# Moving a load ring's slots by 32 bytes in SBUF: from 992 to 0 past a multiple of 1 KB

## The chip, the cores and the metric

One core of a Trainium2 chip. The metric is the device time of one execution, in microseconds; a time quoted is the median of several executions. Most executions of one kernel lie within 0.3% of each other. A page of the profile covers about 2 us less than the device time (191.7 for 193.6).

## The reference, cut to what matters

One decode step of a mixed block: attention of 8 sequences over the last 1024 cached keys and values of 8 heads (16 query heads of 256), an MLP, and a gate that mixes both. What matters here is bytes: keys and values are 67 MB, all data 77.7 MB, and each byte is used once.

```python
W = min(4096, max(256, Sk // 4))                       # 1024
k = jnp.repeat(k_cache[:, :, Sk - W:, :], rep, axis=1)
v = jnp.repeat(v_cache[:, :, Sk - W:, :], rep, axis=1)
p = _softmax(jnp.einsum("bhqd,bhkd->bhqk", q, k) * (Dh ** -0.5), axis=-1)
o = jnp.einsum("bhqk,bhkd->bhqd", p, v)
# ... projection by wo, layernorm + MLP by w1 and w2, g * a + (1 - g) * b
```

## The kernel before

Everything large comes in through a ring of nine slots of 16 KB in each of the 128 partitions. One queue issues the loads in a fixed order, as slots come free: keys of unit 0, wq, w1, w2, then keys and values by turns (2 MB each: 128 rows of 16 KB, one per partition), wo last. Small things go to a pool `consts` that is laid out ahead of the ring in each partition.

```python
    SLOT = 8192            # bf16 elements: 16 KB
    RING = 9
    consts = ctx.enter_context(tc.tile_pool(name="consts", bufs=1))
    ring = ctx.enter_context(tc.tile_pool(name="ring", bufs=RING))
    ktpool = ctx.enter_context(tc.tile_pool(name="ktpool", bufs=3))
    # ... (cut)
    def pump():
        while len(slots) < min(len(plan), consumed[0] + RING):
            t = ring.tile([P, SLOT], BF16, tag="slot", name="slot")
            plan[len(slots)](t)
            slots.append(t)

    def done(n=1):
        consumed[0] += n
        pump()

    def kv_loader(src, u, parts):
        # ... (cut)
        def load(t):
            n = NCK * Dh // parts
            for i in range(parts):
                nc.sync.dma_start(
                    t[:, i * n : (i + 1) * n], v[:, :, i * n : (i + 1) * n]
                )
        return load
    # ... (cut)
    x_sb = consts.tile([NB, D], BF16)
    pump()
    nc.scalar.dma_start(x_sb[:], xf)
    gw_b = consts.tile([NB, D], BF16)
    # ... some forty more small tiles of consts (cut)
```

In the built program all of `consts` lies below the ring, and the slots begin at 44000, 60384, ... 175072 in each partition: 992 past a multiple of 1024, or 224 past a multiple of 256.

## Time and profile before

| | before |
|---|---|
| time, median of 3 | 193.72 us |
| span of the profile | 191.7 us |
| DMA engines busy, 46 to 164 us | 1.00 to 1.01 |
| stream, 46 to 164 us | 426 to 427 GB/s |
| last load lands | 187.1 us |
| VectorE busy, TensorE busy | 67%, 69% |

The views are shown and read in the prediction below. Beside them I use the records of single DMA packets in the trace: one per row moved, with its size, start and duration. Two durations must be kept apart: the recorded one (614 ns for most 16 KB rows), and the spacing of rows on one engine, a few ns less because records overlap.

### The profile page before, as it was taken

To read this page: it belongs to the slowest core of one execution; us is meant where nothing else is said; L and a number is where in the kernel's file an instruction comes from. 1 tells how busy PE (TensorE), PEld (TensorE's weight loads), DVE (VectorE), ACT (ScalarE), POOL (GpSimd) and SP (SyncE) were. 2 spreads that over 40 slices of the span, in tenths; PEclk is the share of its full clock that TensorE was granted. 3 is DMA by queue.
4 is the path that set the end of the run, shared out by engine and by line. 5 is a ranking of instruction groups with operands and counts; after the bars stand their busy time and mean duration, and the time that the engine had idled before them with its cause. 6 is when DMAs were issued, how large, how long until landed. Compare 5 with 4: busy or idle time off the path is not lost.

```text
span 191.7 us, 2514 instructions
## 1 busy us (share of the span) xinstructions
PE 132.8 (69%) x1017; PEld 69.4 (36%) x1026; DVE 128.6 (67%) x189; ACT 45.1 (24%) x93; POOL 5.0 (3%) x7
## 2 busy tenths in 40 slices
PE   0046899894877578865657589958684989386671
PEld 0031783441434243423232254414331534154260
DVE  7867265995949494949494949494959585876201
ACT  2031220214040404140404003403140044045101
POOL 8100000000000000000000000000000000000000
PEclk9999999999699965999999658979998599999555
DMA  5999999999999999999999999999999999999970
GB/s 196 416 412 439 423 419 432 420 420 438 431 420 434 417 427 434 420 427 431 420 434 429 417 431 427 427 427 420 431 427 420 434 427 424 431 426 415 406 307 3
DMA packets 6702, 77.85 MB, mean 406 GB/s; under 512 B 913, under 2 KB 1186, under 8 KB 1954
## 3 DMA queue, kind: packets, MB, share of 16 engines
q1 hardware_dynamic: 6496, 77.67, 96.1%
q8 instruction: 8, 0.13, 0.3%
q10 hardware_dynamic: 194, 0.02, 0.1%
q14 instruction: 4, 0.03, 0.0%
HBM read 77.68 MB, written 0.01 MB: 405 GB/s over the span
## 4 chain that ended last, share of the span: by engine, by line
DMA 96%; SPq 1%; issue 0%; PE 0%; ACT 0%; DVEq 0%; DVE 0%; ACTq 0%
DMA slot<-in_A_k_cache_dram 77%; DMA slot<-in_A_wo_dram 12%; DMA slot<-in_A_wq_dram 7%; SPq L118 1%; SPq L134 0%; PE A_ps L684 0%; ACT res L707 0%; DVEq L735 0%; DVE res L705 0%; ACTq L707 0%
## 5 line engine op out<-in xcount | busy, mean ns | idle before, releaser
L364 DVE STREAM_TRANSPOSE kt<-slot 128x2048 int32<-128x2048 int32 x32 | 73.7, 2305 | 34.6 <-DMA slot<-in_A_k_cache_dram 34.6
L436 PE MATMUL S<-kt,qw 128*128 128x512 bf16 x256 | 70.6, 422 | 30.5 <-DVE kt L364 26.9
L436 PEld LDWEIGHTS <-qw 128*128 128x128 bf16 x256 | 26.6, 104 | 68.0 <-issue 47.9
L541 ACT ACTIVATE oT<-fin,gg_s 128x16 bf16<-128x16 f32 x16 | 5.3, 329 | 76.8 <-PE fin L538 76.8
L465 ACT ACTIVATE E<-S,nmx 128x1024 bf16<-128x1024 f32 x16 | 22.3, 1392 | 2.8 <-DVE nmx L462 2.8
L508 PE MATMUL PO<-slot,ET 128*16 128x512 bf16 x256 | 20.0, 441 | 1.1 <-DMA slot<-in_A_v_cache_dram 1.1
L448 DVE TENSOR_REDUCE mx<-S 128x1 f32<-128x1024 f32 x16 | 19.0, 1184 | 0.0
L517 ACT ACTIVATE first<-PO,own 128x256 f32<-128x256 f32 x16 | 7.6, 474 | 30.2 <-PE PO L508 30.2
L478 DVE STREAM_TRANSPOSE ET<-E 128x512 int32<-128x512 int32 x16 | 11.2, 697 | 2.2 <-ACT E L465 2.2
L456 PE MATMUL mz<-m,same 128*128 128x4 f32 x32 | 6.6, 278 | 5.5 <-ACT oT L541 5.4
L430 PE MATMUL S<-place,foreign 128*128 128x512 bf16 x23 | 9.0, 390 | 0.1
L489 PEld LDWEIGHTS den<-rowsum,rowden 128*128 128x128 f32 x32 | 7.0, 223 | 3.7 <-issue 1.4
L456 PEld LDWEIGHTS mz<-m,same 128*128 128x128 f32 x32 | 5.4, 211 | 7.4 <-ACT oT L541 6.6
L508 PEld LDWEIGHTS <-ET 128*16 128x16 bf16 x256 | 5.5, 94 | 6.4 <-issue 3.3
L430 PEld LDWEIGHTS <-foreign 128*128 128x128 bf16 x32 | 3.2, 100 | 9.4 <-issue 7.6
L489 PE MATMUL den<-rowsum,rowden 128*128 128x1 f32 x32 | 5.0, 226 | 0.4 <-ACT E L465 0.4
L421 DVE CAST qw<-qp 32x512 bf16<-32x512 f32 x4 | 2.7, 687 | 3.4 <-ACT qw L419 3.4
L500 ACT ACTIVATE rsel<-sel,rb 128x8 f32<-128x8 f32 x16 | 4.7, 291 | 1.0 <-DVE rb L499 1.0
L378 PE MATMUL Sq<-slot,xT 128*8 128x512 bf16 x32 | 3.9, 616 | 1.2 <-DMA slot<-in_A_wq_dram 1.2
L684 PE MATMUL A_ps<-slot,oP 128*8 128x112 bf16 x128 | 3.8, 290 | 1.3 <-DMA slot<-in_A_wo_dram 1.3
L462 DVE TENSOR_REDUCE nmx<-mz 128x1 f32<-128x4 f32 x16 | 2.3, 143 | 3.1 <-PE mz L456 3.1
L294 POOL MEMSET qw<- 128x5120 bf16 x1 | 4.4, 4367 | 0.0
(142 smaller groups left out, 90.4 us busy)
## 6 DMA issues: line engine op xcount, KB each, us to landing
slot<-in_A_v_cache_dram SPq DMA_DIRECT2D x16, 2048.0 KB, 37.2
slot<-in_A_k_cache_dram SPq DMA_DIRECT2D x15, 2048.0 KB, 39.1
slot<-in_A_wo_dram SPq DMA_DIRECT2D x3, 896.0 KB, 32.4
slot<-in_A_k_cache_dram SPq DMA_DIRECT2D x2, 1024.0 KB, 7.3
slot<-in_A_wq_dram SPq DMA_DIRECT2D x1, 2048.0 KB, 11.5
slot<-in_B_w_dram SPq DMA_DIRECT2D x1, 1568.0 KB
slot<-in_B_w_dram SPq DMA_DIRECT2D x1, 1344.0 KB
slot<-in_A_wq_dram SPq DMA_DIRECT2D x1, 1024.0 KB, 13.4
```

The lines of the kernel that those rows point to most:

```text
L364: nc.vector.transpose(kt[:].rearrange("p c k x r -> p (c k x r)").bitcast(WORD), kn[:, hf * CH * Dh : (hf + 1) * CH * Dh].bitcast(WORD),)
L430: nc.tensor.matmul(S[u][:, cols], lhsT=foreign[:], rhs=place[:], start=True, stop=False)
L436: nc.tensor.matmul(S[u][:, cols], lhsT=qw[:, j, u, m * RQ : m * RQ + P], rhs=kt[:, :, k, :, par], start=False, stop=(k == NK - 1 and par = ...
L448: nc.vector.reduce_max(mx[:], S[u][:], axis=AXIS.X)
L456: nc.tensor.matmul(mz[:], lhsT=same[:], rhs=m4[:], start=True, stop=True)
L465: nc.scalar.activation(E[:].rearrange("p c x i -> p c i x"), S.pop(u)[:].rearrange("p (c i x) -> p c i x", i=PAIR, x=BLK), ACT.Exp, bias=n ...
L478: nc.vector.transpose(ET[:].rearrange("p c r i -> p (c r i)").bitcast(WORD), E[:].rearrange("p c x i -> p (c x i)").bitcast(WORD),)
L489: nc.tensor.matmul(den[u][:], lhsT=rowden[:], rhs=rowsum[:], start=True, stop=True)
L500: nc.scalar.activation(rsel[u][:], sel2[:], ACT.Copy, scale=rb[:])
L508: nc.tensor.matmul(PO[32 * t : 32 * t + PAIR * RQ], lhsT=ET[:, c, 0:RQ, :], rhs=vn[:, PAIR * c * Dh : PAIR * (c + 1) * Dh], start=(c < QUA ...
L517: nc.scalar.activation(first[:], PO[:, 0, :], ACT.Copy, scale=own[:, 0:1])
L541: nc.scalar.activation(oT[:, half * RQ : (half + 1) * RQ, :, b].rearrange("p h j -> p j h"), sm[:], ACT.Copy, scale=gg_s[:, 1 + b : 2 + b],)
```

## The change

The intent is that rows written by the loads begin at an even address. A tile of 32 B that nobody uses is put first in `consts`, so the ring begins at 44032 = 43 x 1024. A side effect: every other tile in `consts` and behind the ring moves by 32 B too.

```diff
+    consts.tile([P, 16], BF16, name="pad")
     x_sb = consts.tile([NB, D], BF16)
     pump()
```

## The prediction

> **What bounds the kernel now.** I read four views in this order: the strip of 40 slices, the chain of work that ended last, the waits, and the same figures by stage. The strip first, because it tells at a glance whether one resource is full throughout.
>
> ```profile
> PE   0046899894877578865657589958684989386671
> DVE  7867265995949494949494949494959585876201
> DMA  5999999999999999999999999999999999999970
> GB/s 196 416 412 439 423 419 432 420 420 438 431 420 434 417 427 434 420 427 431 420 434 429 417 431 427 427 427 420 431 427 420 434 427 424 431 426 415 406 307 3
> DMA packets 6702, 77.85 MB, mean 406 GB/s; under 512 B 913, under 2 KB 1186, under 8 KB 1954
> ```
>
> The reader is to see that the row of the 16 DMA engines is at 9 tenths from the second slice to the thirty-eighth, and that no compute engine is. From the chain of waits:
>
> ```profile
> ## 4 chain that ended last, share of the span: by engine, by line
> DMA 96%; SPq 1%; issue 0%; PE 0%; ACT 0%; DVEq 0%; DVE 0%; ACTq 0%
> DMA slot<-in_A_k_cache_dram 77%; DMA slot<-in_A_wo_dram 12%; DMA slot<-in_A_wq_dram 7%; SPq L118 1%; SPq L134 0%; PE A_ps L684 0%; ACT res L707 0%; DVEq L735 0%; DVE res L705 0%; ACTq L707 0%
> ```
>
> 96% of the span is loads into the ring that follow one another. The last load lands at 187.13 us in the same chain told in order of time; only 4.6 us (191.7 less 187.1) of last matmuls, copies and the output's store come after it. The waits say who is kept waiting, and the stages how full the stream is (the columns after the busy times are the granted TensorE clock, the DMA engines' busy share and GB/s):
>
> ```profile
> DVE kt L364 <- DMA slot<-in_A_k_cache_dram: 34.6, 14, 2.8
> ...
> PE S L436 <- DVE kt L364: 26.9, 12, 3.1
> ```
>
> ```profile
> 46.00:85.00 39.00, 29.12 (x167) 14.04 (x168) 28.04 (x32) 9.31 (x20) 0.00 (x0) 0.87 1.00 426
> 85.00:125.00 40.00, 28.37 (x166) 13.86 (x168) 28.28 (x33) 9.31 (x20) 0.00 (x0) 0.87 1.00 426
> 125.00:164.00 39.00, 29.11 (x166) 14.04 (x168) 27.81 (x33) 9.29 (x20) 0.00 (x0) 0.87 1.01 427
> ```
>
> VectorE's transposes of the keys wait for keys, TensorE's scores wait for the transposes, and from 46 to 164 us the stream runs at 426 to 427 GB/s with the engines busy all the time. So the time is what the 16 DMA engines take per byte, and a change matters only if it changes that.
>
> **What the Trainium skill says.** "DMA: Bandwidth & Descriptors", section "Where 436 GB/s comes from", puts the ceiling at 16 ports x 32 B x 850 MHz = 435.2 GB/s. The trace's 426 to 427 is 98% of it: about 2% is lost and nothing more can be won. The same page, section "How a descriptor splits into AXI transactions", says that a descriptor goes out in transactions of 256 B, each of which must start at a multiple of 256 B; one that starts 224 B past such a multiple first costs a full transaction of which 32 B are used, and a shorter leftover at the end. "SBUF — State Buffer", section "Operand start alignment", says that its rule on starts is about what is legal and that its runs timed nothing. The same page, section "SBUF: two separate sides", says that DMA and engine ports do not contend; nothing in this trace speaks against it, as the stages above show one rate while the engines' load varies.
>
> **The change, part by part.** It declares a tile of 16 bf16 (32 B in each partition) that no instruction reads or writes. The instruction order of the built program is the same on TensorE but for numbers in names, and no instruction, wait or DMA is added: the counts of the groups will be the same. What moves is addresses. In the built programs the nine slots begin at 44000 + 16384 i in each partition before, and at 44032 + 16384 i after; 44000 is 42 x 1024 + 992, or 224 B past a multiple of 256; 44032 is 43 x 1024. All 275 other listed tiles' addresses, uses of the slots included, rise by 32 B too. The sources in HBM stay where they were.
>
> First the most that it can bring if the skill's account of split transactions holds for the write side as it stands. A row of 16384 B is 512 beats of 32 B. Started 224 B past a multiple of 256 it would be 8 (the first transaction) + 63 x 8 + 7 = 519 beats. A beat at 850 MHz is 1.18 ns, so 7 beats are 8.2 ns per row. The trace's packet records on the load queue have 4096 rows of 16384 B, 384 of 8192, 384 of 7168, and 128 each of 12544, 10752, 4096, 3584, 2688, 1792 and 896 B, 5760 in all and 360 for each of 16 engines: 360 x 8.2 ns = 2.96 us. It would all lie on the path that sets the end, as 96% of that path is loads. 193.72 - 2.96 = 190.8 us, 1.5% less. That is an upper estimate, by that page.
>
> Then whether the records look as if those 7 beats were paid. The usual time of one packet in the trace is 614 ns for 16384 B, 309 for 8192, 159 for 4096, 74 for 1792 and 41 for 896. Without any loss they would be 602.4, 301.2, 150.6, 65.9 and 32.9 (bytes / 27.2 per ns): 7.8 to 8.4 ns more in the last four, which looks just like 7 beats. But a packet's record overlaps the next: two successive starts on one engine lie some 3 to 4 ns closer than the recorded time (613 ns recorded, 609 between starts; 74 recorded, 70 between starts). So the cost of a short packet is nearer 4 ns than 8, less than 7 beats of 1.18. And the trace holds a comparison of its own: the eight rows of gate_w, 896 B each, land at 17408 = 17 x 1024, a whole multiple of 1 KB, and each took 41 ns; the last pieces of wo, also 896 B, begin 96 B past a multiple of 256 (and their source 128 B past one), and 120 of 128 took 41 ns as well. An aligned start has saved nothing there. I take from this that writes into SBUF pay for the bytes, and a small fixed cost, wherever they start. The weakness of this comparison is that gate_w is read from one row over and over, and that 896 B say little about rows of 16 KB.
>
> What the 16 KB rows have beyond twice a row of 8 KB is left: 614 - 602.4 = 11.7 against 7.8 ns, 3.9 ns more. If the crossed boundaries cause that part alone, it is 256 rows per engine x 3.9 ns = 1.0 us. In about a quarter of these packets 621 ns are seen instead, some two of the eight that an engine moves for one load; that goes with the jump in partition and source after four rows, and a shift of all starts by 32 B leaves the jump in place.
>
> The sum, by my main reading: 0 us from the stream, 0 from instructions, so 193.7 us. Weighed with the other cases below it comes to 193.5.
>
> **Rivals.** (1) Split transactions are paid on the write side: 190.8 us as worked out. For it: 426 x 519 / 512 = 432, close under the ceiling, so the lost 2% would be mostly explained. Against it: the 896 B rows, and the 1792 B rows whose spacing of 70 ns is 60 beats where 63 would be due. (2) Only long rows pay, 1.0 us: 192.7. For it is only that the 16 KB rows are worse than twice 8 KB; against it, that the source's jumps explain such things as well. (3) The moved engine operands get slower or faster. Every one was at a multiple of 32 B before and is at one after, so I expect 2305 ns for the keys' transposes again; and if they were 5% slower (32 x 0.115 = 3.7 us of VectorE), VectorE waits 34.6 us for keys and has that room: 193.7. (4) A worse pattern, with more writes of one moment in the same part of the memory, now that rows begin evenly: slots are 16384 B apart before as after, and the rows of all partitions start at one offset in both, so the pattern only moves; it would cost, and nothing in the profile asks for it.
>
> **Range and chances.** No change seen, 193.5 to 193.9: some 72%. Rival 2 or a part of it, 192.2 to 193.4: 14%. Rival 1, 190.5 to 191.5: 9%. The rest is slower by a little or something unknown. Eight times in ten that gives 191.4 to 194.0. Faster by over 2% means under 189.85, so 3.87 us from the stream of about 185 us; at 426.5 GB/s that needs 426.5 x 185 / 181.1 = 435.6, above the ceiling: 2%. Slower by over 2% needs a loss for which I see no source: 1%. Within 2%: 97%.
>
> **What would show each step right or wrong.** Right: 426 to 427 GB/s again from 46 to 164 us, 614 ns for most 16 KB packets, 309 for 8 KB ones, the chain still 96% loads with the last landing near 187.1 us, keys' transposes at 2305 ns. The gate_w rows, which lose their even start (17440 after the change), stay at 41 ns. Rival 1 would show 605 to 606 ns for 16 KB and a stream near 432 GB/s, rival 2 some 610 ns and 429. A time under 190 us would mean that the ceiling is not what holds the stream; one above 195 that placement in SBUF costs writes or reads in a way that I don't see.

## The result, and the profile after

| | before | after |
|---|---|---|
| time, median (range) | 193.69 us (193.35 to 193.83), 4 runs | 191.52 us (191.41 to 191.56), 4 runs |
| after / before | | 0.989 (95%: 0.987 to 0.991) |
| once more, on another occasion | 193.41 us, 9 runs | 191.68 us, 5 runs; 0.991 (0.990 to 0.993) |

A ratio here is the mean time of one kernel's fast runs over that of the other's fast runs of the same rounds, so it isn't quite the ratio of the medians. The gain is about 1%, some 1.7 to 2.2 us: inside the 2% band, and clear of noise.

The profile after, in the same views. The strip:

```profile
DMA  5999999999999999999999999999999999999980
GB/s 195 417 432 426 428 439 427 432 425 425 442 425 435 425 425 439 425 439 429 425 432 427 439 429 422 439 425 435 429 425 439 429 429 429 429 434 421 415 338 4
```

The chain of waits:

```profile
## 4 chain that ended last, share of the span: by engine, by line
DMA 81%; PE 9%; DVE 6%; SPq 1%; ACT 1%; issue 1%; DVEq 0%; ACTq 0%
```

and its end in order of time (start, duration, what):

```profile
123.19 38.80 DMA slot<-in_A_k_cache_dram
162.02 23.02 DMA slot<-in_A_wo_dram
185.03 0.04 issue
```

The stages (columns as in the prediction: length, busy time of TensorE, weight loads, VectorE, ScalarE, GpSimd, granted clock, DMA share, GB/s):

```profile
46.00:85.00 39.00, 28.34 (x166) 13.85 (x168) 27.98 (x33) 9.29 (x20) 0.00 (x0) 0.87 1.01 431
85.00:125.00 40.00, 29.11 (x166) 14.07 (x168) 29.02 (x33) 9.30 (x20) 0.00 (x0) 0.87 1.01 429
125.00:164.00 39.00, 30.13 (x166) 14.37 (x168) 28.17 (x33) 9.30 (x20) 0.00 (x0) 0.82 1.01 431
```

and the costliest groups and waits of VectorE after (busy, mean ns | idle before):

```profile
L365 DVE STREAM_TRANSPOSE kt<-slot 128x2048 int32<-128x2048 int32 x32 | 73.7, 2306 | 31.8 <-DMA slot<-in_A_k_cache_dram 31.8
```

Before, the line of the transposes and the last landing were:

```profile
L364 DVE STREAM_TRANSPOSE kt<-slot 128x2048 int32<-128x2048 int32 x32 | 73.7, 2305 | 34.6 <-DMA slot<-in_A_k_cache_dram 34.6
187.13 0.04 issue
```

The reader is to see four things. The DMA row is as full as before, but the same busy share now moves 429 to 431 GB/s in place of 426 to 427. The last load lands at 185.03 us instead of 187.13; from there to the end nothing has changed (4.6 us in both). The transposes of keys take 2306 ns (2305 before), so the moved tiles did nothing for VectorE; it only waits less for keys, 31.8 us after 34.6. And the chain names less DMA (81% for 96%): in its first 45 us it now goes through TensorE and VectorE, since a slot was set free by them a little later than a landing. The stages from 46 us on still have the DMA engines full.

The packet records say where the time went. Recorded durations of rows on the load queue:

| row | before: usual (share), mean | after: usual (share), mean |
|---|---|---|
| 16384 B (keys, values, half of wq) | 614 (2214 of 4096) and 619 to 621 (1112), 617.0 | 611 (4064 of 4096), 612.1 |
| 12544 B (w2) | 473 (75 of 128), 477.1 | 469 (all), 469.0 |
| 7168 B (wo) | 275 (150 of 384), 278.4 | 272 (382 of 384), 273.3 |
| 2688 B (wo) | 107 (31 of 128), 111.1 | 107 (all), 107.0 |
| 10752 B (w1) | 404 (109 of 128), 404.5 | 404 (all), 404.0 |
| 4096 B (wq) | 159 (all), 159.0 | 159 (all), 159.0 |

In every load of the first 19 us (the first keys, wq, w1) the usual row is as long before as after; from w2 on the rows of every load have become shorter in the mean, if hardly so the last ones of 896 B. Counting bytes landed against time from the first packet says the same: 9 MB are in 0.1 us earlier after the change, 40 MB 1.0 us, 74 MB 1.6 us, 77.6 MB 1.8 us. It is a gain by the row, nearly all the way; only the last 0.07 MB, in this pair of traces, bring 0.3 us more at once.

### The profile page after: what moved, and what is told of

The parts are those of the page before. It is cut to its first block, busy times and chain, and to the rows that moved or that the text cites. A ratio compares the mean times of both kernels' runs of the same rounds, so it can differ in the third digit from the quotient of the medians.

```text
span 189.6 us, 2514 instructions
## 1 busy us (share of the span) xinstructions
PE 134.6 (71%) x1017; PEld 70.2 (37%) x1026; DVE 128.8 (68%) x189; ACT 45.0 (24%) x93; POOL 5.0 (3%) x7
## 4 chain that ended last, share of the span: by engine, by line
DMA 81%; PE 9%; DVE 6%; SPq 1%; ACT 1%; issue 1%; DVEq 0%; ACTq 0%
DMA slot<-in_A_k_cache_dram 62%; DMA slot<-in_A_wo_dram 12%; DMA slot<-in_A_wq_dram 7%; PE S L437 4%; DVE kt L365 4%; PE hT L565 2%; PE hT L555 1%; DVE mx L449 1%; SPq L118 1%; SPq L134 1%; PE Sq L379 1%; PE qt L394 1%; ACT qs L389 1%; PE qp L407 1%; DVE ET L479 0%
## 5 line engine op out<-in xcount | busy, mean ns | idle before, releaser
L365 DVE STREAM_TRANSPOSE kt<-slot 128x2048 int32<-128x2048 int32 x32 | 73.7, 2306 | 31.8 <-DMA slot<-in_A_k_cache_dram 31.8
L437 PE MATMUL S<-kt,qw 128*128 128x512 bf16 x256 | 72.1, 430 | 27.7 <-DVE kt L365 24.3
```

The source lines that it names most:

```text
L365: nc.vector.transpose(kt[:].rearrange("p c k x r -> p (c k x r)").bitcast(WORD), kn[:, hf * CH * Dh : (hf + 1) * CH * Dh].bitcast(WORD),)
L437: nc.tensor.matmul(S[u][:, cols], lhsT=qw[:, j, u, m * RQ : m * RQ + P], rhs=kt[:, :, k, :, par], start=False, stop=(k == NK - 1 and par = ...
```

## The experiments

Ten runs were made; the last is the changed kernel once more. Those with computing gave right results; those with loads alone are wrong.

### Nine starts in one kernel: stagger

```diff
-    SLOT = 8192
+    SLOT = 8192 + 16
```

> Each slot is 32 B longer, so the nine slots begin 992, 0, 32, 64, 96, 128, 160, 192 and 224 B past a multiple of 1 KB, all in one kernel. Theory A (a row's start decides, and 64 B is the boundary that counts): rows of 16 KB into the slots at 0, 64, 128 and 192 take 611 ns each as after the change, those at 992, 32, 96, 160 and 224 take 614 or 621 as before; the time lies between, about 192.6 us. Theory B (the boundary is 256 B or more): only the slot at 0 has rows of 611 ns, and the time is 193.4 us. Theory C (not the ring's rows but other moved tiles matter): all slots alike.

Measured: 192.95 us beside 193.32 (ratio 0.998, 0.997 to 1.000). The trace's rows by slot, from the middle of each load:

| slot begins, past 1 KB | 0 | 32 | 64 | 96 | 128 | 160 | 192 | 224 | 992 |
|---|---|---|---|---|---|---|---|---|---|
| usual row, ns | 611 | 611 | 613 | 612 | 611 | 612 | 613 | 614 | 614 |
| mean of rows under 640 ns | 611.2 | 611.8 | 615.0 | 614.5 | 613.7 | 614.2 | 615.0 | 615.9 | 615.7 |

In the built program the slots are filled, after the first round, in the order 224, 192, 992, 160, 128, 0, 32, 64, 96. Theory C (engines' tiles) falls, because slots of one kernel differ. Theory A in its form with 64 B falls as well: 64 and 192 are as slow as their neighbours. But the slot at 32 is fast, where no theory had it. It is filled right after the slot at 0; what that means came out later.

### Another uneven start: pad64

```diff
-    consts.tile([P, 16], BF16, name="pad")
+    consts.tile([P, 32], BF16, name="pad")
```

> 64 B of filling in place of 32: every slot begins 32 B past a multiple of 1 KB, and past one of 64. Theories A and B, where a start off the boundary costs: as before the change, 193.5 us, with rows of 614 and 621 ns. Theory D (any move away from 992 helps, because the last 32 B ahead of a boundary are the bad place): 191.5 us, rows of 611 ns.

Measured: 193.58 us beside 193.32 (ratio 1.0015, 0.9998 to 1.003), 2213 rows of 614 ns and 1107 of 619 to 621: the kernel before, over again.

```profile
46.00:85.00 39.00, 28.67 (x159) 13.90 (x157) 27.77 (x32) 7.30 (x16) 0.00 (x0) 0.81 1.00 426
```

So it isn't the move that helps but where it ends. And a start at 32 is slow when all slots have it, though it was fast in the mixed kernel.

### The loads alone: loads_before and loads_after

All computing is taken out; the loads, their order and their addresses stay (the result is wrong).

```diff
     x_sb = consts.tile([NB, D], BF16)
     pump()
+    consts.tile([P, 12848], BF16, name="rest")     # the ring at 44000 as before
+    for _ in range(len(plan)):
+        done()
+    res = consts.tile([NB, D], BF16)
+    nc.vector.memset(res[:], 0.0)
+    nc.sync.dma_start(out_f, res[:])
-    ... all the rest of the kernel
```

The second has the 32 B of filling as well.

> Wrong result on purpose: every load of the kernel before, to the same addresses, and no computing at all (zeros go out). If the cost lies in the DMA engines' own writes, rows of 16 KB still take 614 and 621 ns after the first 20 us. If it is a contest with the compute engines for SBUF, they take 611 ns throughout.

> The same loads alone with the slots 32 B further on, at multiples of 1 KB. Rows of 611 ns under every theory; the whole stream some 2 us shorter than in the loads alone of before if the cost is the DMA engines' own, and equal to it if it is a contest with the compute engines.

Measured: 188.38 and 186.60 us, one run each. The page of each, its first line and its stages (VectorE and GpSimd idle, clock, DMA share, GB/s). At 44000:

```profile
span 186.6 us, 93 instructions
...
46.00:85.00 39.00, 0.00 (x0) 0.00 (x0) 1.00 1.00 426
85.00:125.00 40.00, 0.00 (x0) 0.00 (x0) 1.00 1.01 428
```

At 44032:

```profile
span 184.8 us, 93 instructions
...
46.00:85.00 39.00, 0.00 (x0) 0.00 (x0) 1.00 1.01 432
85.00:125.00 40.00, 0.00 (x0) 0.00 (x0) 1.00 1.01 431
```

With no engine at work, 16 KB rows show 614 (2221 of 4096) and 619 to 621 ns (1114) at 44000, while those of wq, in the first 18 us, are still at 611; and 611 (4081) at 44032. The difference of 1.8 us, from one run of each, is as large as that of the whole kernels (1.7 to 2.2), and the rows bear it out. It is the DMA engines' own: nothing of it comes from engines and loads getting in each other's way, and nothing from the engines' moved tiles. The start without the cost is there too (here the rows of w1 already pay: 404 ns in only 15 of 128), so no engine's work starts it. This agrees with the Trainium skill, "SBUF — State Buffer", section "SBUF: two separate sides", which the prediction cites: the usual 16 KB row is 614 ns with all engines at work and with none.

### Phases of one start each: phases

With loads alone there is room for more. One kernel of 176 loads of 2 MB (wrong), in phases of 8:

```python
for dst, src in PHASES:                 # bytes past a multiple of 1 KB in SBUF, bytes early in HBM
    for _ in range(8):
        t = ring.tile([P, SLOT + 512], BF16, tag="slot", name="slot")
        v = # ... 128 rows of 16 KB of keys or values, from src bytes before their start
        nc.sync.dma_start(t[:, dst // 2 : dst // 2 + SLOT], v)
```

> Wrong result on purpose: only loads of 2 MB with rows of 16 KB, in 22 phases of 8 loads, each phase with its own start of rows in SBUF (bytes past a multiple of 1 KB) and in HBM: 0, 224, 0, 32, 0, 64, 0, 96, 0, 128, 0, 160, 0, 192, 0, 224, 256 (HBM start even), then 0 with the HBM start 32 B early, 0, 32 with HBM 32 early, 0, 224 with HBM 224 early. Theory A2 (the row that starts off a multiple of 256 B is sent in 65 pieces of up to 256 B in place of 64, and a piece under 128 B costs as 128 B): usual row 611 ns at 0, 128 and 256, 612 at 96 and 160, 613 at 64 and 192, 614 at 32 and 224, the early rows of each phase still at 611 if a store of bytes in the engine must fill first. Theory A1 (64 B is the boundary): 611 at 0, 64, 128, 192, 256 and 614 at the others. Theory B2 (512 B or 1 KB is the boundary): 256 is slow too. If the start in HBM relative to that in SBUF is what counts, the phases with both shifted alike are at 611 and the one with HBM alone shifted is slow.

Measured, for the second half of each phase; spacing is the time in which 384 rows landed, times 16 engines, over 384, so it includes the small completion writes (4 B, 9 ns each in the records):

| start in SBUF | start in HBM | usual row late in the phase, ns | spacing per row, ns |
|---|---|---|---|
| 0 (after another phase) | even | 611 (all) | 607.8 |
| 256 | even | 611 (all) | 607.8 |
| 32; 224 | even | 614, two in eight 621 | 613.0; 613.0 |
| 64; 192 | even | 613, two in eight 620 | 611.9; 611.9 |
| 96; 160 | even | spread over 611 to 619 | 611.8; 611.5 |
| 128 | even | 615, 619 and 611 | 611.8 |
| 0 | 32 early | 611 (all) | 607.8 |
| 32 | 32 early | 614, two in eight 621 | 613.0 |
| 224 | 224 early | 614, two in eight 621 | 613.0 |

An even phase that held a disturbed row of 905 ns is left out. The first uneven phase, at 224 right after the start-up, is an exception: its rows were disturbed (up to 702 ns), yet 611 stayed the usual one to its end (400 of its last 512). I can't explain it.

Three things follow. The boundary is 256 B: a start at 256 is as good as one at a multiple of 1 KB. The start in HBM costs nothing, neither by itself nor relative to that in SBUF. And any start off 256 B costs 3.7 to 5.2 ns a row. Theory A2, that a short piece costs as much as one of 128 B, is right only about the small differences (32 and 224 are 1 ns worse than the rest); a start at 128 leaves no short piece and should have been at 611, but costs 4 ns. So the largest step is in being off the boundary at all.

In each uneven phase but the first, nearly all rows stay at 611 for three to four loads before the cost shows: some 28 rows of an engine at 32 and 224, some 35 at 64 to 192 (an engine has about 8 of a load's 128 rows).

### 256 is enough, 128 isn't: pad288 and pad160, in the whole kernel

```diff
-    consts.tile([P, 16], BF16, name="pad")
+    consts.tile([P, 144], BF16, name="pad")      # pad160: [P, 80]
```

> 288 B of filling: the slots begin 256 B past a multiple of 1 KB. If 256 B is the boundary, as fast as the change (191.3 us, ratio to before 0.989, rows of 611 ns); if 512 B or 1 KB is, as before (193.4 us, rows of 614 and 621).

> 160 B of filling: the slots begin 128 B past a multiple of 256 B. Theory A2: one piece more per row but no short piece, so between the two kernels, about 192.5 us, usual row 611 to 612 ns with two in eight at 619. If 128 B is boundary enough: 191.3 us. If only the missing 256 B count, all alike: 193.4 us.

Measured beside the same runs of before (193.69 us): pad288 191.89 us, ratio 0.991 (0.990 to 0.992), 4062 of 4096 rows at 611 ns; pad160 193.39 us, ratio 0.999 (0.997 to 1.002), rows all over 611 to 621, in the mean 615.8. Stages of pad288, then of pad160:

```profile
46.00:85.00 39.00, 26.48 (x168) 12.78 (x169) 28.11 (x33) 9.29 (x20) 0.00 (x0) 0.96 1.01 431
```

```profile
46.00:85.00 39.00, 28.68 (x170) 14.05 (x170) 27.93 (x32) 9.55 (x22) 0.00 (x0) 0.87 1.01 428
```

The expected halfway time of pad160 was a miss: it saves 0.3 us at the median, not one half, and its interval includes no gain at all.

### Everything but the ring: all_but_ring

The 32 B go in as in the change; 32 B are taken out further on in `consts`, by putting two small tiles into one, and 32 B are put in behind the ring. So the slots stay at 44000. In the built program everything behind the ring and all of `consts` ahead of the two merged tiles move as in the change; the seven tiles of `consts` that follow these two stay where they were.

```diff
+    gap = ctx.enter_context(tc.tile_pool(name="gap", bufs=1))       # behind the ring
+    consts.tile([P, 16], BF16, name="pad")
+    gap.tile([P, 16], BF16, name="pad2")
-        gl = consts.tile([NB, 1], F32)
+        gl2 = consts.tile([NB, 2], F32)
+        gl, gth = gl2[:, 0:1], gl2[:, 1:2]
-        gth = consts.tile([NB, 1], F32)
```

> Every other tile moves by 32 B as in the change, the nine slots stay at 44000 and so on. If the rows of the ring are the cause: as before, 193.4 us, rows of 614 and 621 ns. If the engines' own tiles or the small loads gain from the move: 191.3 us.

Measured: 193.80 us beside 193.69 (ratio 1.001, 0.999 to 1.002), 2219 rows of 614 ns. The places of the tiles that moved are worth nothing. (One of its five runs, the profiled one, from which the rows are, took 195.54 us, with a slower start, 390 GB/s in the second slice of the strip, and a longer end; the other four took 193.7 to 193.9.)

### Mixed starts and shorter rows: phases2

Loads alone, as in the phases above, but with longer phases, starts by turns, and rows of 8 and 4 KB.

```python
PHASES = [   # loads, starts by turns, elements in a row
    (8, [0], 8192), (24, [224], 8192), (24, [0, 224], 8192), (24, [224, 224, 224, 0], 8192),
    (8, [0], 8192), (24, [224], 4096), (24, [0], 4096), (48, [224], 2048), (48, [0], 2048),
]
```

> Wrong result on purpose: loads alone again, in phases: 8 loads of 16 KB rows at an even start (a multiple of 1 KB), 24 at 224 past it, 24 with 0 and 224 by turns, 24 with three at 224 and one at 0 by turns, 8 at 0; then 8 KB rows, 24 loads at 224 and 24 at 0; then 4 KB rows, 48 at 224 and 48 at 0. If each row that starts off the boundary leaves the engine's writes a little behind its reads, and even rows let them catch up: 614 ns from the fifth load of the first long phase on; by turns 0 and 224 all at 611 ns or nearly so; three to one in between. If the cost goes by the load alone: in the mixed phases the rows at 224 take 614 and 621 and those at 0 take 611. If it is paid per row, rows of 8 KB and 4 KB lose about 5 ns each as well (309 to 312 and 319, 159 to 162 and 168), twice and four times as much per byte; if per byte, 2.5 and 1.2 ns each.

Measured in the second half of each phase:

| rows | starts | spacing per row, ns | over the even one |
|---|---|---|---|
| 16 KB | 0 | 607.8 | |
| 16 KB | 224 | 612.8 | 5.0 |
| 16 KB | 0 and 224 by turns | 608.9 | 1.1 (2.1 per uneven row) |
| 16 KB | three at 224, one at 0 | 611.5 | 3.7 (4.9 per uneven row) |
| 8 KB | 0 / 224 | 306.6 / 311.7 | 5.1 |
| 4 KB | 0 / 224 | 156.0 / 160.0 | 4.0 |

The cost is per row, nearly whatever its length. Loads with uneven rows stay at the fast rate at first: the means over the middle of each load of the first uneven phase are 611.0, 611.0, 611.0, 613.7, then 615.8 ns, those of the phase with 8 KB rows 309.0, 309.0, 309.0, 311.5, then 314.8 to 315.0. I call this the grace: it is some 28 rows of an engine in both, and 33 to 37 with 4 KB, so it goes by rows much more than by bytes. (Expected were the fifth load for its end, which came in the fourth, and 611 ns by turns, which was nearly so.) And even loads give some of it back: by turns, an uneven row costs 2.1 ns instead of 5.0; with three uneven to one even, the load right after the even one is at 612.7 and the next two at 615.8. This explains the fast slot at 32 in the mixed ring, and the first 19 us of the kernel before, which are the first 48 rows of each engine. What is stored and given back inside the engine, no record shows; that its writes fall behind its reads a little with each uneven row is a guess that fits.

### The change once more: after_again

The changed kernel again, with no edit.

> The changed kernel once more, for the size of the effect beside more runs of the kernel before: ratio 0.988 to 0.991, 191.3 to 191.9 us.

Measured: 191.68 us beside 193.41, ratio 0.991 (0.990 to 0.993), 4078 of 4096 rows at 611 ns.

## Why the prediction was right or wrong, point by point

The time lies inside the predicted range (191.4 to 194.0), near its lower end. That was a hedge and some luck: the main reading, no change, with 72% of the weight, was wrong, and 191.52 lies just outside the 190.5 to 191.5 of rival 1 (9%). The weights put on the two rivals are what kept the range wide enough.

- **What bounds the kernel: right.** The stream does, from 3 us to the end; what was won in it (last landing 2.1 us earlier) came out at the end in full.
- **No instruction changes, engines gain nothing: right.** 2306 ns for 2305, and all_but_ring is at 1.001.
- **"Writes into SBUF pay for the bytes, and a small fixed cost, wherever they start": this is the step that failed.** In its place the runs show 3.7 to 5.2 ns for each row of 16 KB that starts off a multiple of 256 B. The reading rested on rows of the first 20 us (8192, 4096, 1792 B, gate_w), most of which fall in the grace, when an uneven start costs nothing yet. The short rows late in the trace told otherwise: 2688 B took 107 to 121 ns before and 107 after. The 896 B rows of gate_w and of wo's end were no test: by the account of transactions that the prediction takes from the Trainium skill, I estimate four transactions for such a row at each of the starts compared (0, 32, 96 and 128 B past 256), so none was split off; and wo's last piece starts 128 B past 256 after the change too. The 1792 B rows hide a cost in another way: the first rows of w2, right behind them, took 490 to 505 ns in 13 cases before and in 16, one per engine, in loads_before, against 473 for most and 469 for all after. It looks as if what short rows owe is recorded on the next row; no run tests this.
- **"It goes with the jump in partition and source after four rows, and a shift of all starts leaves the jump in place": wrong.** Rows of 619 to 621 ns went from 1112 to 2. The jump may pick out which two of eight rows suffer, but they suffer only with uneven starts.
- **Rival 1, split transactions paid on the write side: the side was right, the size too large, and the beats are not what is paid.** Counted as the prediction counts them, an estimate from the skill's account, a start at 32 would cost 1 beat more (513 for 512), 1.2 ns, and one at 224 7 beats, 8.2 ns; measured are 5.2 ns for both (phases). Every uneven start has one transaction more (65 for 64), which fits better, but nothing here shows that it is the cause. The term was 360 rows an engine at 8.2 ns, 2.96 us. Measured is 5.0 ns a row of 16 KB, and the first 48 rows or so of the 360 pay nothing: 312 x 5.0 = 1.6 us. The records give the same: the sum of packet durations on the load queue per engine fell from 184.29 to 182.67 us, by 1.6. Against that stand 1.8 us in the loads alone and 1.7 to 2.2 us in the whole kernel. The 0.1 to 0.6 us beyond are of the size of the scatter between runs of before; 0.3 us of them, in the pair of traces above, come in the last 0.07 MB.
- **Rival 2, only long rows pay: wrong.** Rows of 8 KB pay as much as those of 16 KB. They looked cheap because all of them were loaded in the first 20 us.
- **The signs.** The usual 16 KB row came to 611 ns, as rival 2 had it (610), and the stream to 429 to 431 GB/s, between rival 2 (429) and rival 1 (432). The gate_w rows, moved off their even start, stayed at 41 ns as forecast; being among the first rows, and with no transaction more by the estimate above, they could not have shown a cost.
- **The ceiling: it held.** With even starts a 16 KB row is spaced at 607.8 ns, 16384 x 16 / 607.8 = 431.3 GB/s, under the 435.2 of the Trainium skill ("DMA: Bandwidth & Descriptors", section "Where 436 GB/s comes from"), so a gain over 2% was out of reach. The same section says that loads from HBM are bound lower, at some 358 GB/s; the 426 to 432 GB/s measured here, with one core at work, are above that, so it was right to go by 435.2.

## What to carry to other kernels

In a kernel bound by loads, let the rows that land in SBUF begin at multiples of 256 B: it costs a few bytes of filling, and in the loads alone here gave 0.8% of the load time with rows of 16 KB, 1.7% with 8 KB (5.1 of 306.6 ns), 2.6% with 4 KB (4.0 of 156.0). Starts in SBUF depend on what else is allocated ahead of them, so they change without anyone meaning it; look them up in the built program. And when a record of one stage is used as evidence for another, check that the stage is in the same steady state: the first loads here hid the cost.

## What the Trainium skill lacked or had wrong

- "DMA: Bandwidth & Descriptors", section "How a descriptor splits into AXI transactions", gives the rule by which the prediction counts beats for uneven starts: 519 for 512 with the rows here, an estimate of 8.2 ns at 850 MHz. The runs show 5.0 ns for 16 KB and 8 KB rows and 4.0 for 4 KB at 224 past 256 B, and 3.7 to 5.2 ns for any start off it that was tried, as much at 32 (1 beat) as at 224 (7 beats), on the side of SBUF only. A start 32 B early in HBM cost nothing (607.8 ns either way).
- The same page's "Rules for kernel authors" has no rule on the start of rows in SBUF; the runs show 256 B as the boundary (rows of 611 ns at 0 and 256, 614 and 621 at 32 and 224), worth 1% of this kernel.
- "SBUF — State Buffer", section "Operand start alignment", treats legality and says that its runs timed nothing; 426 to 428 GB/s at 44000 and 431 to 432 at 44032 in the loads alone could be put beside it.
- None of the pages has it that an uneven start costs nothing for some 28 to 37 rows of an engine after even ones, and that even loads give part of this back (2.1 ns per uneven row by turns, 5.0 without even ones).
